# A diffusion-transformer block on one core: more dummy matmuls and wider scale matmuls ahead of the key projection, and a later gate load

## The chip, the cores and the metric

One core of a Trainium2 chip runs the whole kernel. The metric is the device time of one execution in microseconds; for a kernel the median of several runs is given. A profile is of one execution.

## The reference, cut to what matters

The block works on x (2 batches, 256 tokens each, width 1152) with a condition c (2 x 1152). All inputs are bf16.

```python
mod = (_silu(c) @ w_mod).reshape(B, 6, 1, D)
shift_a, scale_a, gate_a, shift_m, scale_m, gate_m = [mod[:, i] for i in range(6)]
h = _layernorm(x, axis=-1) * (1 + scale_a) + shift_a
qkv = (h @ wqkv).reshape(B, N, 3, H, Dh)
...
a = jnp.einsum('bhqk,bkhd->bqhd', attn, v).reshape(B, N, D) @ wo
x = x + gate_a * a
h2 = _layernorm(x, axis=-1) * (1 + scale_m) + shift_m
m = _gelu(h2 @ w_fc1) @ w_fc2
return x + gate_m * m
```

The change concerns scale_a (a product of silu(c), two rows, with a 1152 x 1152 part of w_mod), the key projection that follows it, and the load of the weights of gate_a.

## The kernel before, in words

Weights are cut into 9 slabs of 128 rows ("k-tiles"), tokens into 4 tiles of 128. Everything is recorded first as units with reads and writes; a small planner then gives each engine its order. The order of TensorE (pe) and of the DMA queue of SyncE (sp) is the order of the program text; DVE and ACT follow a list written by hand (`S.first`) at the start of the kernel and the planner's priorities behind it. Helpers record every operation: all ordinary matmuls stand on L692 (`mm`), all transposes on L695 (`tr`), all DMAs on L673 (`dma`), copies on L687 (ACT) and L689 (DVE).

The start of TensorE's order is:

1. `warm_a` (7 dummies), the transpose of c, `warm(5, "b")`. A dummy is a matmul of the identity with a zero tile of 512 columns into PSUM bank 2 (bank 7 for "a"); nothing reads its result.
2. `sca_one`: a matmul of ones that puts the 1 of (1 + scale_a) into PSUM bank 7 and bank 3. Then `sca_0`, `sca_1`, `warm(4, "c")`, `sca_2` to `sca_4`. `mod_kt` does one k-tile: for each of the five 128-wide column blocks f = 0 to 4 (`KC` = 5) it takes a 128 x 128 piece of the scale weights as the stationary operand and moves two columns, silu(c) of the two batches (`ST[:, kt:18:9]`, two elements 9 apart). Block 0 accumulates in bank 3, blocks 1 to 4 in bank 7. The other four blocks of scale_a come later, in unit `scb`, with the roles of the operands changed.
3. `xnT_1`, `xnT_0`: 9 transposes each of the normalised token tiles 1 and 0.
4. `sca_first`: block 0 for k-tiles 5 to 8; then DVE copies the first transposed k-tile (`xnT_cp0_0`) and multiplies it by the scale (`hk_0_0`, L831). Then `sca_5` to `sca_8` for blocks 1 to 4. `sc1a` (L819) copies the scales from PSUM to `SC1A`.
5. The key projection of batch 0: units `k0_<pair>_<k-tile>`, each two matmuls of 256 columns, k-tiles 0 to 4, with the transposes of tile 2 behind k-tile 1 and those of tile 3 (`xnT_3a`, `xnT_3b`) inside k-tile 4; then batch 1, `scb`, k-tiles 5 to 8, the shift (`sh`), the queries, scores, values, attention, the output projection and the MLP.

Token tile 3 is loaded behind the second key slab. DVE takes its statistics (L740, L741, L743), POOL its power (L744), and DVE normalises it in two parts (L771, 640 and 512 columns), which `xnT_3a` and `xnT_3b` read.

SyncE's queue holds, in order: x, the first scale weights (4 loads), key slabs 0 and 1, token tile 3, key slabs 2 to 4, the other scale weights (3 loads), key slabs 5 to 8, the shift weights (3 loads), then the query slabs 0 to 8 with the first gate load `ga_load(0)` behind slab 1, and what follows. The query slabs go where the scale weights were, so they wait for `scb`; the place of the gate weights (`WMODR`) is free from the start. DVE computes gate_a from them (`attn_gate`, L1061 for k-tile 0 and L1064 for the others); the result goes through a scratch buffer in DRAM and comes back as a row that L1165 multiplies with.

Of the kernel before, what the change touches and what calls it, by code (L numbers as in the profile page):

```python
# [497 lines left out]
P = 128  # L498
NTOK = 512
D = 1152  # L500
KT = 9
# [8 lines left out]
KC = 5  # L510
# [33 lines left out]
def build_kernel(nc, x, c, wqkv, wo, w_mod, w_fc1, w_fc2, out):  # L544
# [5 lines left out]
    with (  # L550
# [4 lines left out]
        def sb(off, nbytes, dt=BF16):  # L555
            assert off % 4 == 0 and off + nbytes <= ARENA_BYTES, (off, nbytes)
            v = arena[:, off // 2:(off + nbytes) // 2]
            if dt == F32:
                v = v.bitcast(F32)
            return v  # L560

        def ps32(bank, c0=0, n=512):
            return psum[:, bank * 512 + c0: bank * 512 + c0 + n]

        def ps16(bank, c0=0, n=1024):
            v = psum[:, bank * 512: (bank + 1) * 512].bitcast(BF16)
            return v[:, c0:c0 + n]
# [15 lines left out]
        def misc(nbytes):  # L583
            o = mo[0]
            mo[0] += (nbytes + 3) // 4 * 4
            assert mo[0] <= ARENA_BYTES
            return o
# [22 lines left out]
        Q4B = sb(O_Q4B, 1024)  # L610
# [21 lines left out]
        IDENT = sb(misc(256), 256)  # L632
        ONES = sb(misc(256), 256)
# [3 lines left out]
        ST = sb(misc(36), 36)  # L637
# [5 lines left out]
        SC1A = sb(misc(72), 72, F32)  # L643
# [27 lines left out]
        def dma(dst, src, nbytes, name, is_out=False, eng="sp", run=4096):  # L671
            eff = 1.0 if run >= 4096 else (1.08 if run >= 2304 else (1.15 if run >= 1536 else (1.3 if run >= 1024 else 1.42)))
            return S.op(eng, 500.0 if eng == "sp" else 150.0, lambda e: e.dma_start(dst, src), reads=[src], writes=[dst],  # L673
                        name=name, dma_bytes=nbytes * eff, is_out=is_out)

        def dve(cost, fn, reads, writes, name):
            return S.op("dve", cost, fn, reads=reads, writes=writes, name=name)
# [7 lines left out]
        def copy_on(eng, dst, src, n, psum16, name):  # L685
            if eng == "act":
                act(c_act(n), lambda e: e.activation(out=dst, in_=src, func=ACTF.Copy), [src], [dst], name)  # L687
            else:
                return dve(c_dve_psum16(n) if psum16 else c_dve_psum32(n), lambda e: e.tensor_copy(dst, src), [src], [dst], name)  # L689

        def mm(o, l, r, st, sp, **kw):
            S.instr(lambda e: e.matmul(o, lhsT=l, rhs=r, start=st, stop=sp, **kw), reads=[l, r], writes=[o])  # L692
# [62 lines left out]
        for t in range(4):  # L755
# [5 lines left out]
            m = MV[:, t, 0:1]  # L761
# [14 lines left out]
        def xt_ps(b, kt, n=1):  # L776
            if b == 0:
                return (4, 5, 6)[kt // 4], (kt % 4) * 256
            return (7, (kt - KC) * 256) if kt >= KC else ((6, 4)[kt % 2], kt // 2 * 256)

        def xn_T(t, part="", kts=range(KT)):
            b = t // 2
            S.unit("pe", len(kts) * c_mm(128), "xnT_%d%s" % (t, part))
            for kt in kts:
                bank, c0 = xt_ps(b, kt)
                tr(ps16(bank, c0 + (t % 2) * 128, 128), XN[:, t, kt * 128:(kt + 1) * 128], IDENT)

        def xn_T_copy(b, kts, eng):
            bank, c0 = xt_ps(b, kts[0])
            n = len(kts)  # L790
            src = ps16(bank, c0, n * 256).rearrange("p (k t) -> p k t", k=n)
            st = kts[1] - kts[0] if n > 1 else 1
            copy_on(eng, HX[:, kts[0]:kts[-1] + 1:st, b * 256:(b + 1) * 256], src, n * 256, True, "xnT_cp%d_%d" % (b, kts[0]))

        def warm(n, tag):
            for i in range(n):
                S.unit("pe", 215.0, "warm_%s_%d" % (tag, i))
                mm(ps32(2), IDENT, Q4B, True, True)

        def mod_kt(W, kt, col0, name, fs=(0, 9)):  # L800
            if name:
                S.unit("pe", (fs[1] - fs[0]) * 27.0, name)
            for f in range(*fs):
                mm(ps32(7 if f else 3, col0 + f * 2, 2), W[:, kt, f * 128:(f + 1) * 128], ST[:, kt:18:9], False, kt == KT - 1,
                   skip_group_check=True)

        def quads(w, g0, g1, q):
# [7 lines left out]
                   skip_group_check=not fresh)  # L815

        def sc1a(ka, kb):
            m, o = ps32(7 if ka else 3, 2 * ka, 2 * (kb - ka)), SC1A[:, 2 * ka:2 * kb]
            dve(170, lambda e: e.tensor_copy(o, m), [m], [o], "sc1a_%d" % ka)  # L819


        def hk(kt, b, eng="dve"):
            dst, s1 = HK[:, kt, b * 256:(b + 1) * 256], SC1A[:, kt * 2 + b:kt * 2 + b + 1]
            if kt + b == 0:
                s1 = ps32(3, 0, 1)
            bank, c0 = xt_ps(b, kt)
            src = ps16(bank, c0, 256) if kt < KC and kt + b > 0 else HX[:, kt, b * 256:(b + 1) * 256]
            if eng == "act":
                act(c_act(256, 1), lambda e: e.activation(out=dst, in_=src, func=ACTF.Copy, scale=s1), [src, s1], [dst], "hk_%d_%d" % (kt, b))
                return  # L830
            dve(256 if kt < KC else 200, lambda e: e.tensor_scalar(out=dst, in0=src, scalar1=s1, scalar2=None, op0=ALU.mult),  # L831
                [src, s1], [dst], "hk_%d_%d" % (kt, b))
# [10 lines left out]
        def k_pair(kts, i, b, bank=None):  # L843
            S.unit("pe", 2 * len(kts) * c_mm(256), "k%d_%d_%d" % (b, i, kts[0]))
            bank = KB[b][i] if bank is None else bank
            if kts[0] == 0:
                for kt in kts:
                    for half in range(2):
                        k_mm((kt,), 2 * i + half, b, bank, half)
            else:  # L850
                for half in range(2):
                    k_mm(kts, 2 * i + half, b, bank, half)
            if kts[-1] == KT - 1:
                eng = "act" if ev_rr[0] % 2 == 0 else "dve"
                ev_rr[0] += 1
                copy_on(eng, QK[:, 9 + 2 * i:11 + 2 * i, b * 256:(b + 1) * 256], ps32(bank).rearrange("p (j t) -> p j t", j=2), 512, False,
                        "k_ev%d_%d" % (b, i))

        warm(5, "b")
        S.unit("pe", 27.0, "sca_one")  # L860
        mm(ps32(7, 0, 2 * KC), ONES[0:1, :], ONES[0:1, 0:2 * KC], True, False, skip_group_check=True)
        mm(ps32(3, 0, 2), ONES[0:1, :], ONES[0:1, 0:2], True, False, skip_group_check=True)
        for kt in range(0, 2):
            mod_kt(WSC, kt, 0, "sca_%d" % kt, (0, KC))
        warm(4, "c")
        for kt in range(2, 5):
            mod_kt(WSC, kt, 0, "sca_%d" % kt, (0, KC))
        xn_T(1)
# [1 line left out]
        S.unit("pe", 4 * 27.0, "sca_first")  # L870
        for kt in range(5, 9):
            mod_kt(WSC, kt, 0, "", (0, 1))
        xn_T_copy(0, (0,), "dve")
        hk(0, 0)
        sc1a(0, 1)
        for kt in range(5, 9):
            mod_kt(WSC, kt, 0, "sca_%d" % kt, (1, KC))
        sc1a(1, KC)
        for kt in range(1, KC):
            hk(kt, 0, "act" if kt == 4 else "dve")  # L880
        xn_T_copy(0, (8,), "act")
        xn_T_copy(0, (5, 6, 7), "act")
        for kt in range(KC):
            for i in range(2 if kt == KC - 1 else 4):
                k_pair((kt,), i, 0)
            if kt == 1:
                xn_T(2)
# [15 lines left out]
        for c0, c1 in ((0, 32), (32, 32 * (KT - KC))):  # L903
            ka, kb = KC + c0 // 32, KC + c1 // 32
# [9 lines left out]
        def ga_load(k0):  # L914
            dma(WMODR[:, k0:k0 + 3, 0:FG], wmod_v[:, k0:k0 + 3, 2 * D:2 * D + FG], 3 * P * FG * 2, "ld_ga%d" % k0, run=FG * 2)

        for kt in range(KT):
            dma(WQ[:, kt, :], wqkv_v[:, kt, 0:D], P * D * 2, "ld_wq%d" % kt, run=2304)
            if kt == 1:
                ga_load(0)  # L920
        for kt in range(KC, KT - 2):
            for b in range(2):
# [225 lines left out]
        def acc_bank():  # L1148
            b = acc[acc_rr[0] % len(acc)]
            acc_rr[0] += 1  # L1150
            return b
# [125 lines left out]
        for t in range(4):  # L1277
# [4 lines left out]
            for (c0, c1) in pieces:  # L1282
                w = c1 - c0
                S.unit("pe", JT * c_mm(w), "fc2_%d_%d" % (t, c0))
                o = ps32(acc_bank(), 0, w)
# [22 lines left out]
def bass_standalone__dit_block__diffusion_kernel(  # L1308
    nc: bass.Bass,
    x: bass.AP,  # L1310
    c: bass.AP,
    wqkv: bass.AP,
    wo: bass.AP,
    w_mod: bass.AP,
    w_fc1: bass.AP,
    w_fc2: bass.AP,
    out: bass.AP,
):
    build_kernel(nc, x, c, wqkv, wo, w_mod, w_fc1, w_fc2, out)
# [28 lines left out]
```

## Time and profile before

| | |
|---|---|
| median of 3 runs | 242.92 us (242.85 to 243.38) |
| span of the profiled execution, first to last instruction | 242.5 us |
| time of the profiled execution around its span | not given by the page |
| TensorE busy | 237.3 us, 98% of the span |
| mean granted TensorE clock | 0.993 |
| DVE, ACT, POOL busy | 121.5, 67.8, 19.9 us |
| DMA | 51.58 MB, mean 213 GB/s |

Busy time of TensorE is the union of its matmuls, whose ends are modelled; neighbouring matmuls overlap in the records. The granted clock is the share of TensorE's full clock that was let through. A wait in the timeline stands in brackets behind the instruction that it held up, with what ended it.

### The profile page before, as it was taken

Reading aid. Unit: us, or ns where it says so; the run is one execution under the profiler, and the core shown is the slowest. Engines: PE = TensorE matmul, PEld = TensorE weight load, DVE = VectorE, ACT = ScalarE, POOL = GpSimd, SP = SyncE. Lnnn points to the kernel's source line nnn. Section 1 sums busy time; section 2 is a strip of 40 time slices with the busy share of each in tenths; the row PEclk is TensorE's granted clock in tenths of the full one; section 3 lists DMA queues with packets and bytes.
Section 4 is the critical chain, followed back from the end, with each engine's and each line's share of the span. In section 5 each row is a group of like instructions: output and inputs, shape, how many; then the busy total and the mean of one; then the engine's idle time right before and its main releaser. Section 6 shows DMA issues by size and latency. Waiting matters only on the chain.

```text
span 242.5 us, 3957 instructions
## 1 busy us (share of the span) xinstructions
PE 237.3 (98%) x1699; PEld 145.4 (60%) x1699; DVE 121.5 (50%) x229; ACT 67.8 (28%) x136; POOL 19.9 (8%) x36
## 2 busy tenths in 40 slices
PE   6899999999999999999999999999999999999995
PEld 2688844466666666898544444444666566566564
DVE  2654379988996689669999700000022222111112
ACT  4921440435524206973233322222000000000000
POOL 1300000000002276400000110000000000000000
PEclk9979999999999999999999999999999999999999
DMA  6999999999992999999963499100000000000000
GB/s 221 378 370 392 389 392 390 398 413 402 391 352 79 312 374 391 391 348 398 352 198 83 157 313 374 43 0 3 0 16 19 16 16 16 19 16 16 21 27 20
DMA packets 30363, 51.58 MB, mean 213 GB/s; under 512 B 1547, under 2 KB 15755, under 8 KB 30347
## 3 DMA queue, kind: packets, MB, share of 16 engines
q1 hardware_dynamic: 29888, 50.73, 58.9%
q0 software_dynamic: 288, 0.60, 0.8%
q8 instruction: 13, 0.21, 0.4%
q10 hardware_dynamic: 171, 0.01, 0.0%
q14 instruction: 3, 0.02, 0.0%
HBM read 50.15 MB, written 1.19 MB: 212 GB/s over the span
## 4 chain that ended last, share of the span: by engine, by line
PE 95%; DMA 3%; SPq 1%; DVE 0%; issue 0%
PE psum L692 93%; DMA arena<-in_wqkv_dram 3%; PE psum L695 2%; SPq L673 1%; DVE arena L1290 0%; DVE arena L1291 0%
## 5 line engine op out<-in xcount | busy, mean ns | idle before, releaser
L692 PE MATMUL psum<-arena 128*128 128x384 bf16 (+8 forms) x1610 | 234.0, 314 | 2.4 <-POOL arena L718 1.5
L692 PEld LDWEIGHTS psum<-arena 128*128 128x128 bf16 (+2 forms) x1610 | 139.7, 97 | 92.4 <-issue 3.8
L1290 DVE TENSOR_TENSOR arena<-psum,arena 128x384 f32<-128x384 f32 (+2 forms) x13 | 6.8, 526 | 88.6 <-PE psum L692 88.6
L1200 ACT ACTIVATE arena<-psum 128x512 bf16<-128x512 f32 (+1 forms) x45 | 22.8, 512 | 42.1 <-PE psum L692 42.1
L687 ACT ACTIVATE arena<-psum 128x512 bf16<-128x512 f32 (+6 forms) x34 | 18.2, 560 | 37.9 <-PE psum L692 37.9
L1064 DVE SCALAR_TENSOR_TENSOR arena<-arena 128x1152 f32<-128x1152 bf16 x16 | 21.9, 1408 | 0.0
L1095 DVE SCALAR_TENSOR_TENSOR arena<-arena 128x1152 f32<-128x1152 bf16 x16 | 21.4, 1414 | 0.0
L1166 POOL TENSOR_TENSOR arena<-arena 128x384 f32<-128x384 f32 x12 | 10.9, 912 | 11.7 <-DVE arena L1165 9.5
L740 DVE BATCH_NORM_STATS2 arena<-arena 128x6 f32<-128x384 f32 (+1 forms) x18 | 9.5, 549 | 3.8 <-DMA arena<-in_x_dram 3.8
L673 POOL DMA_DIRECT2D dit_scratch<-arena x4 | 2.4, 609 | 96.6 <-DVE arena L1082 60.3
L689 DVE CAST arena<-psum 128x512 bf16<-128x512 f32 x11 | 7.2, 687 | 5.3 <-PE psum L692 5.3
L1165 DVE TENSOR_TENSOR arena<-psum,arena 128x384 f32<-128x384 f32 x12 | 6.7, 556 | 3.7 <-PE psum L692 3.7
L1171 ACT ACTIVATE arena<-arena 128x1152 bf16<-128x1152 f32 x4 | 5.4, 1344 | 9.8 <-DVE arena L1170 9.8
L695 PE MATMUL psum<-arena 128*128 128x128 bf16 (+1 forms) x89 | 7.4, 225 | 0.4 <-DMA arena<-in_c_dram 0.4
L695 PEld LDWEIGHTS psum<-arena 128*128 128x128 bf16 (+1 forms) x89 | 6.3, 102 | 2.2 <-DMA arena<-in_c_dram 1.1
L1291 DVE TENSOR_TENSOR arena<-arena 128x384 bf16<-128x384 f32 (+2 forms) x13 | 6.9, 527 | 0.5
L1190 ACT ACTIVATE arena<-psum,arena 128x128 bf16<-128x128 bf16 x16 | 6.1, 455 | 3.0 <-PE psum L695 2.2
L1187 DVE TENSOR_SCALAR arena<-psum,arena 128x128 bf16<-128x128 bf16 x20 | 5.5, 336 | 2.9 <-PE psum L695 2.9
L1009 ACT ACTIVATE arena<-psum,arena 128x256 bf16<-128x256 f32 x8 | 3.7, 471 | 0.2 <-DVE arena L1006 0.2
L744 POOL TENSOR_TENSOR arena<-arena 128x1 f32<-128x1 f32 x6 | 3.3, 555 | 4.7 <-DVE arena L743 4.5
L1005 DVE TENSOR_REDUCE arena<-psum 128x2 f32<-128x512 f32 x4 | 2.8, 688 | 0.9 <-PE psum L692 0.7
L962 ACT ACTIVATE arena<-arena 128x256 bf16<-128x256 bf16 x6 | 2.5, 495 | 1.5 <-DVE arena L956 1.5
(60 smaller groups left out, 53.9 us busy)
## 6 DMA issues: line engine op xcount, KB each, us to landing
arena<-in_w_fc_dram SPq DMA_DIRECT2D x9, 1152.0 KB, 8.0
arena<-in_w_fc_dram SPq DMA_DIRECT2D x4, 2592.0 KB, 17.6
arena<-in_wqkv_dram SPq DMA_DIRECT2D x18, 288.0 KB, 9.3
arena<-in_w_mod_dram SPq DMA_DIRECT2D x6, 864.0 KB, 12.3
arena<-in_w_mod_dram SPq DMA_DIRECT2D x3, 1728.0 KB, 20.5
arena<-in_wqkv_dram SPq DMA_DIRECT2D x1, 2592.0 KB, 17.6
arena<-in_wo_dram SPq DMA_DIRECT2D x1, 2592.0 KB, 24.9
arena<-in_w_mod_dram SPq DMA_DIRECT2D x1, 2592.0 KB, 18.5
```

What stands on the lines that cost most here:

```text
L687: act(c_act(n), lambda e: e.activation(out=dst, in_=src, func=ACTF.Copy), [src], [dst], name)
L689: return dve(c_dve_psum16(n) if psum16 else c_dve_psum32(n), lambda e: e.tensor_copy(dst, src), [src], [dst], name)
L692: S.instr(lambda e: e.matmul(o, lhsT=l, rhs=r, start=st, stop=sp, **kw), reads=[l, r], writes=[o])
L695: S.instr(lambda e: e.transpose(o, i_, idn), reads=[i_, idn], writes=[o])
L740: dve(550, lambda e, s=s, o=o: e.bn_stats(out=o, in_=s), [s], [o], "bn_%s_%d" % (tag, ci))
L1064: ga_units[(b, kt)] = dve(150 + FG * 1.1, lambda e, o=o, w=w, s1=s1: e.scalar_tensor_tensor(out=o, in0=w, scalar=s1, in1=o, op0=ALU.mult, ...
L1095: u = dve(1300, lambda e, o=o, w=w, s1=s1: e.scalar_tensor_tensor(out=o, in0=w, scalar=s1, in1=o, op0=ALU.mult, op1=ALU.add), [w, s1, o], ...
L1165: dve(550, lambda e, o=o, ga=ga, x1c=x1c: e.tensor_tensor(out=x1c, in0=o, in1=ga, op=ALU.mult), [o, ga], [x1c], "wo_t1_%d_%d" % (t, ci))
L1166: S.op("pool", 930, lambda e, xs=xs, x1c=x1c: e.tensor_tensor(out=x1c, in0=x1c, in1=xs, op=ALU.add), reads=[x1c, xs], writes=[x1c], name=" ...
L1200: act(c_act(ntok), lambda e: e.activation(out=dst, in_=o, func=ACTF.Gelu_apprx_tanh), [o], [dst], "gelu_%d_%d" % (f, tok0))
L1290: dve(c_dve_psum32(w), lambda e, o=o, gm=gm, t1=t1: e.tensor_tensor(out=t1, in0=o, in1=gm, op=ALU.mult), [o, gm], [t1], "fc2_t1_%d_%d" % ( ...
L1291: dve(c_dve_32(w), lambda e, t1=t1, x1c=x1c, ost=ost: e.tensor_tensor(out=ost, in0=t1, in1=x1c, op=ALU.add), [t1, x1c], [ost], "fc2_out_%d ...
```

## The change

- In `mod_kt` each scale matmul moves 64 columns: the two columns of silu(c) repeated 32 times by a dimension of step zero. Each block f then has 64 columns of PSUM of which the first two are read. `sca_one` is widened to match, and `sc1a` reads two columns of every 64.
- `warm(4, "c")` becomes `warm(7, "c")`; one dummy goes into `sca_first`, behind k-tile 7 and ahead of k-tile 8; one (`warm(1, "d")`) goes ahead of the first matmul of the key projection.
- `ga_load(0)` is issued behind query slab 4 in place of query slab 1.

```diff
         def mod_kt(W, kt, col0, name, fs=(0, 9)):
...
-                mm(ps32(7 if f else 3, col0 + f * 2, 2), W[:, kt, f * 128:(f + 1) * 128], ST[:, kt:18:9], False, kt == KT - 1,
+                mm(ps32(7 if f else 3, f * 64, 64), W[:, kt, f * 128:(f + 1) * 128], ST[:, kt:18:9].unsqueeze(1).broadcast_to([P, 32, 2]), False, kt == KT - 1,
                    skip_group_check=True)
...
         def sc1a(ka, kb):
-            m, o = ps32(7 if ka else 3, 2 * ka, 2 * (kb - ka)), SC1A[:, 2 * ka:2 * kb]
+            m = ps32(7 if ka else 3, 64 * ka, 64 * (kb - ka)).rearrange("p (f c) -> p f c", c=64)[:, :, 0:2]
+            o = SC1A[:, 2 * ka:2 * kb].rearrange("p (f c) -> p f c", c=2)
...
-        mm(ps32(7, 0, 2 * KC), ONES[0:1, :], ONES[0:1, 0:2 * KC], True, False, skip_group_check=True)
-        mm(ps32(3, 0, 2), ONES[0:1, :], ONES[0:1, 0:2], True, False, skip_group_check=True)
+        ones64 = ONES[0:1, 0:64].unsqueeze(1)
+        mm(ps32(7, 0, 64 * KC), ONES[0:1, :], ones64.broadcast_to([1, KC, 64]), True, False, skip_group_check=True)
+        mm(ps32(3, 0, 64), ONES[0:1, :], ONES[0:1, 0:64], True, False, skip_group_check=True)
         for kt in range(0, 2):
             mod_kt(WSC, kt, 0, "sca_%d" % kt, (0, KC))
-        warm(4, "c")
+        warm(7, "c")
...
         for kt in range(5, 9):
             mod_kt(WSC, kt, 0, "", (0, 1))
+            if kt == 7:
+                mm(ps32(2), IDENT, Q4B, True, True)
...
         xn_T_copy(0, (5, 6, 7), "act")
+        warm(1, "d")
         for kt in range(KC):
             for i in range(2 if kt == KC - 1 else 4):
                 k_pair((kt,), i, 0)
...
             dma(WQ[:, kt, :], wqkv_v[:, kt, 0:D], P * D * 2, "ld_wq%d" % kt, run=2304)
-            if kt == 1:
+            if kt == 4:
                 ga_load(0)
```

## The prediction

> **What bounds the kernel now.** I read the page first: the busy line, the granted clock and the chain that ended last.
>
> ```profile
> span 242.5 us, 3957 instructions
> ...
> PE 237.3 (98%) x1699; PEld 145.4 (60%) x1699; DVE 121.5 (50%) x229; ACT 67.8 (28%) x136; POOL 19.9 (8%) x36
> ...
> PEclk9979999999999999999999999999999999999999
> ...
> PE psum L692 93%; DMA arena<-in_wqkv_dram 3%; PE psum L695 2%; SPq L673 1%; DVE arena L1290 0%; DVE arena L1291 0%
> ```
>
> TensorE carries 95% of the chain; the 3% in front of it is one transfer, the first key weights, landing at 10.76 us. After that PE never waits, so a microsecond taken from PE early in the kernel reaches the end, unless a transfer or another engine's result is not early enough. The clock row has one low digit after the start, a 7 in the third slice (12.1 to 18.2 us). I cut that region into equal stretches with the windows view (columns: length; PE busy and instructions; granted clock; DMA share; GB/s):
>
> ```profile
> 4.32:7.73 3.41, 2.96 (x23) 1.00 0.99 339
> 7.73:11.15 3.42, 2.67 (x58) 1.00 1.04 389
> 11.15:14.56 3.41, 3.41 (x22) 0.50 1.06 388
> 14.56:17.97 3.41, 3.41 (x40) 1.00 1.09 363
> ```
>
> From 11.15 to 14.56 PE has half its clock, and there it is busy without a break with K matmuls. Then PE's timeline (start, length, operation, count):
>
> ```profile
> 8.35 0.55 PE L692 MATMUL psum<-arena 128*128 128x2 bf16 x15 [0.53 <-DMA arena<-in_w_mod_dram]
> 8.76 1.17 PE L695 MATMUL psum<-arena 128*128 128x128 bf16 x18
> 9.76 0.88 PE L692 MATMUL psum<-arena 128*128 128x2 bf16 x20
> 10.81 3.31 PE L692 MATMUL psum<-arena 128*128 128x256 bf16 x16 [0.16 <-DMA arena<-in_wqkv_dram]
> 13.90 0.98 PE L695 MATMUL psum<-arena 128*128 128x128 bf16 x9
> 14.72 2.35 PE L692 MATMUL psum<-arena 128*128 128x256 bf16 x20
> 16.91 0.44 PE L695 MATMUL psum<-arena 128*128 128x128 bf16 x5
> 17.19 0.38 PE L692 MATMUL psum<-arena 128*128 128x256 bf16 x2
> 17.41 0.39 PE L695 MATMUL psum<-arena 128*128 128x128 bf16 x4
> 17.63 2.89 PE L692 MATMUL psum<-arena 128*128 128x256 bf16 x31
> ```
>
> Durations overlap, so costs come from start to start. At full clock: 2 columns (8.76-8.35)/15 = 27 ns; 128-column transposes (9.76-8.76)/18 = 55.6 ns; 256 columns (16.91-14.72)/20 = 109.5 ns; 512 columns 214 to 216 ns (the windows view has 187 records, two of them cut, in the 40 us from 125 to 165). At half clock, the 16 K matmuls from 10.81 to 13.90 are three at 109 ns and 13 at 212 ns.
>
> **Why the clock fell.** In time spent streaming columns, the stretch 4.32 to 7.73 holds nine 512-column dummies and the end of a tenth, 9 x 0.215 + 0.17 = 2.1 us, 62% of it, and the clock stayed. The stretch 7.73 to 11.15 holds 35 matmuls of 2 columns (35 x 0.8 ns = 0.03), 18 transposes (1.0) and three K matmuls (0.33): 40% with the transposes, 11% without. The clock then fell. What keeps it lies between 40 (or 11) and 62%.
>
> Whether transposes count no row separates, so I carry both sums.
>
> **The change, part by part.** *64 columns in place of 2.* No row has 64 columns. Bounds: 27 ns (2 columns) and 55.6 ns (128 columns). I take 29 ns: the step from 128 to 256 columns is 0.42 ns a column, so 64 are 26.9 ns, plus the 2 ns by which 128 columns exceed 53.8. There are 45 (10, 15, 4 and 16), so 45 x 2 ns = 0.09 us, part of it before a wait that hides it. The opening ones-matmul grows from 10 to 320 columns (0.14 us) and lies between 6.23 and 6.51, where PE waits for scale weights. The strided read of PSUM in sc1a stays 8 elements a row: nothing.
>
> *Three more dummies in "c"* (4 to 7): PE idles 0.53 us before 8.35 and its last dummy starts at 7.44. With sca_0 and sca_1 2 ns slower each, seven end at 6.82 + 7 x 0.215 = 8.33. The wait hides them; they would cost 0.65 us without it. *One among the first-column matmuls* (0.215): three of those go at once at 9.76, the fourth at 10.05, after its weights. Now it goes at 9.80 + 0.09 + 0.215 = 10.10. *One ahead of K* (0.215): 16 x 29 ns end at 10.60, the dummy at 10.82, and the K weights land at 10.76. The first column's user on DVE moves from 10.36 to 10.4 and is still done by 10.7. So K starts at about 10.83 in place of 10.81. The five dummies cost 0.02 us together because waits of 0.53, 0.2 and 0.25 us lie exactly there.
>
> *The clock.* The stretch 7.73 to 11.15 now streams 0.60 (dummies) + 0.43 + 0.215 + 0.58 + 0.215 + 0.33 = 2.4 us, 69%, and 99% with transposes. Both exceed the 62% that kept the clock, so I forecast 1.00 throughout.
>
> *K at full clock.* From 10.83: 16 x 0.1095 to 12.58; 9 transposes, 0.50, to 13.08 (their input on ACT ends 12.4, some 0.1 later now); the third key weights land at 5.35 + 7.7 = 13.05, the fourth and fifth at 13.8 and 14.5; 20 matmuls, 2.19, to 15.27. Next come the transposes of the last token tile, and here another engine becomes late:
>
> ```profile
> 14.08 0.15 DVE L743 TENSOR_SCALAR arena<-arena 128x1 f32<-128x1 f32 x1
> 14.89 0.77 DVE L771 TENSOR_SCALAR arena<-arena 128x640 bf16<-128x640 bf16 x2 [0.67 <-POOL arena L744]
> 17.39 0.87 DVE L831 TENSOR_SCALAR arena<-psum,arena 128x256 bf16<-128x256 bf16 x3 [1.73 <-PE psum L695]
> ```
>
> The first half of that tile is normalised at 14.89 + 0.45 = 15.34, after a chain that starts with X landing at 12.27 and does not move. With a semaphore PE goes on at 15.42: 0.15 us given back. Then 0.28, 0.22 and 0.22 to 16.14. Before, that point is 17.63: the gain is 1.49 us. (Half of 3.41 is 1.71; less 0.02, 0.15 and rounding.) The DVE row of 17.39 moves with the transposes.
>
> *What must be early enough for that gain.* The last scale weights land at 8.10 + 10.5 = 18.6 and are read in the last third of a stage that moves from 20.2 to 18.7; the sixth key weights at 19.4, wanted at 21.0; the last shift weights at 14.95 + 13.8 = 28.7, wanted in the last third of a stage moving from 30.1 to 28.6, so at 29.3 (the tightest, 0.6 us); the first Q weights at 29.5, wanted at 31.8. Nothing stops the gain.
>
> *Later first gate load.* On SP's queue it goes from behind the second Q load to behind the fifth, so Q loads 3 to 5 are issued earlier and the gate weights (864 KB, landed 21.44 + 11.1 = 32.5) land where the fifth Q load did, 23.81 + 10.9 = 34.7. It waits for nothing, so nothing queues behind it; POOL's queue is untouched. Its first reader, DVE L1061, ran at 35.12 and could run at 33.6; it will start at 34.8, holding back copies and softmax work queued behind it on DVE by up to 1.2 us. DVE's own waits for PE take that back: 0.51 us before 45.14 and 0.72 before 53.36. Price on the path: nothing; without that cover, the gate row would reach its first user (DVE L1165 at 81.59, row landed 80.6) 0.5 us late, with the four PSUM banks of that stage in rotation between it and PE.
>
> **Sum.** The profiled span is 242.5; the median of the runs is 242.92, 0.4 above, the part outside the span, which I leave alone. 242.5 - 1.49 = 241.0 of span, 241.4 of time. The three runs spread 0.5 us, and the profiled one has all of its half-clock stretch inside K, the dearest place; a stretch from 10.15 to 13.56 would cost (13.56 - 10.81)/2 = 1.4 us in place of 1.7. So the median may stand to lose a little less, and I take 241.5. The Trainium skill, "TensorE: Matmul & The Clock Gate", Part 1, says that the clock is halved after an idle window of 3.4 us and restored after a busy one, and that the window runs free of the kernel's start. The 3.41 us at 0.50 agrees; one trace cannot show the free running. By the rule the gain differs from run to run, about 1.0 to 1.5; without it, 1.5 in each.
>
> **Rivals.** *Half-speed operand (0.11).* The repeated operand is two elements 18 bytes apart, read by turns. If that streams at half rate, 64 columns take 55.6 ns like 128. Then sca_0 and sca_1 push the dummies past 8.35, all 45 are on the path, 45 x 27 ns = 1.2 us, and K starts at about 11.95; the wait of 0.15 vanishes, the second transposes' end is at 11.95 + 1.75 + 0.50 + 2.19 + 0.72 = 17.1 against 17.63: 242.4. Against it: nothing shown; for it: no contiguous row either. *Quarter speed (0.06), the slower side.* Same place: each at 107 ns costs 45 x 78 ns = 3.5 us, less the gain of 1.64 (no wait of 0.15): 244.8. It decides from about 65 ns a matmul (29 ns and 1.64 us over 45) and is slower beyond 0.2% from 76 ns. The bound is the 128-column row doubled, 111 ns. The Trainium skill, "Advanced Engine Details and Errata", "SBUF Cachelines", speaks for both: an access that goes to another 16-byte line each time pays a penalty, of no stated size; no run here shows it. *The clock falls all the same (0.09).* If activity is counted otherwise (array cells or useful weights), 0.50 stays in the row and only 0.03 us is added: 242.95. For it: the exact threshold is unknown; against it: 69% against a kept 62%.
>
> **How the numbers follow.** The main case has 0.74. About 0.2% (0.49 us) is what a measurement of this kernel can tell from no change, so faster is below 242.43. The half-speed case straddles that: 0.06 of it is faster, 0.05 is same. Faster 0.74 + 0.06 = 0.80; same 0.05 + 0.09 = 0.14; slower 0.06. The range goes from 241.1 (all 1.71 gained) to 242.6 (half speed with 0.2 more), holding 0.85.
>
> **What would show it.** Right: the clock at 1.00 from 11.15 to 14.56; K's first row at 10.8 to 10.9; 64-column starts 29 ns apart; a PE wait of 0.1 to 0.2 us near 15.3 for DVE; the 31-matmul row near 16.1; L1061 at 34.8. Wrong: 0.50 anywhere in K, a K row near 12, or a new PE wait behind 20 us.

## The result, and the profile after

The changed kernel takes 244.68 us (median of 4 runs, 244.62 to 244.92); the kernel before takes 242.90 (4 runs). The ratio is 1.0074, 95% interval 1.0061 to 1.0088: slower by 1.8 us, where 1.4 us faster was forecast.

With this result came, for each run, its time and its span side by side. The profiled execution of the changed kernel has a span of 243.2 and a time of 244.92; time less span is 1.7 to 1.8 us in every run of both kernels since. So the trace that the prediction was made from, with its span of 242.5, is one of an execution of about 244.25 us, and not of the 242.9 us that it was set beside.

The windows view of the changed kernel, in the same stretches as before (length; PE busy and instructions; granted clock; DMA share; GB/s):

```profile
4.32:7.73 3.41, 3.04 (x12) 1.00 0.97 322
7.73:11.15 3.42, 3.42 (x43) 1.00 1.04 381
11.15:14.56 3.41, 3.36 (x45) 1.00 1.05 393
14.56:17.97 3.41, 3.41 (x40) 1.00 1.09 360
```

This trace holds no clock record at all, so none of its four 1.00 says anything, and only 12 instructions stand in the first row. The half-clock stretch in the key projection (K) is gone all the same, as forecast: its 16 matmuls up to 14.91 follow each other by 109 ns, where 13 of them took 212 ns before. PE's timeline of the changed kernel (start, length, operation, count, wait):

```profile
4.98 0.19 PE L695 MATMUL psum<-arena 18*128 18x18 bf16 x1 [0.29 <-DMA arena<-in_c_dram]
5.10 5.63 PE L692 MATMUL psum<-arena 128*128 128x512 bf16 x39
10.57 1.17 PE L695 MATMUL psum<-arena 128*128 128x128 bf16 x18
11.57 3.51 PE L692 MATMUL psum<-arena 128*128 128x64 bf16 x37
14.91 0.67 PE L695 MATMUL psum<-arena 128*128 128x128 bf16 x9
15.42 2.35 PE L692 MATMUL psum<-arena 128*128 128x256 bf16 x20
17.60 0.44 PE L695 MATMUL psum<-arena 128*128 128x128 bf16 x5
17.88 0.38 PE L692 MATMUL psum<-arena 128*128 128x256 bf16 x2
18.10 0.39 PE L695 MATMUL psum<-arena 128*128 128x128 bf16 x4
18.32 0.93 PE L692 MATMUL psum<-arena 128*128 128x256 bf16 x7
```

There is no wait longer than 0.15 us between 5.1 and 18.3: the waits that were to hide the dummies are gone, and PE is late. Transposes start at 10.57 (8.76 before), K's first matmul is at 13.17 (10.81), and the row forecast near 16.1 is at 18.32. From K's first matmul to that row it is 5.15 us (6.82 before): K does run at full clock. From start to start the 64-column matmuls are 58 to 60 ns apart, not 29.

### The profile page after: what moved, and what is told of

It is laid out like the page before. It is cut to its first block, busy times and chain, and to the rows that moved or that the text cites. A ratio compares the mean times of both kernels' runs of the same rounds, so it can differ in the third digit from the quotient of the medians.

```text
span 243.2 us, 3958 instructions
## 1 busy us (share of the span) xinstructions
PE 238.3 (98%) x1695; PEld 146.5 (60%) x1704; DVE 121.3 (50%) x229; ACT 67.8 (28%) x136; POOL 20.2 (8%) x36
## 4 chain that ended last, share of the span: by engine, by line
PE 96%; DMA 2%; issue 0%; SPq 0%; DVE 0%
PE psum L692 94%; DMA arena<-in_w_mod_dram 2%; PE psum L695 2%; SPq L673 0%; DVE arena L1295 0%; DVE arena L1296 0%
## 5 line engine op out<-in xcount | busy, mean ns | idle before, releaser
L687 ACT ACTIVATE arena<-psum 128x512 bf16<-128x512 f32 (+6 forms) x34 | 18.3, 560 | 39.0 <-PE psum L692 36.8
```

## Experiments

Times are medians; behind each stands the ratio to the kernel before, run beside it on the same chip, with its 95% interval. The letters of theories and rivals are those of the expectations. "Ones" is the matmul of ones ahead of the first scale matmul. Starts of single matmuls are read from the trace, where the rows shown merge several.

**e5_before: the kernel before, for a trace of its usual execution.** No edit.

> The kernel before, unchanged, for a trace of its usual execution. In the comparisons so far 33 of 35 of its executions have a span of 240.9 to 241.6 and two 242.6 to 242.7, and time minus span is 1.7 to 1.8 in all; the trace that the prediction was made from has 242.5 and belongs to the two. Theory F (the trace shown was of a rare execution): K starts near 10.8 us with 109 ns between matmuls from the first to the last, no half-clock stretch behind 8 us, and the last pair of the first batch's K at 16.2 to 16.4, not 17.6; span near 241.2. Rival G (the shorter spans come from somewhere else, later loads or the end): the half-clock stretch is there and the pair stands near 17.6.

243.19 us (1.0007, 0.9988 to 1.0026). The traced execution has a span of 241.4 and a time of 243.20. PE's timeline in it:

```profile
8.72 1.17 PE L695 MATMUL psum<-arena 128*128 128x128 bf16 x18
9.73 0.86 PE L692 MATMUL psum<-arena 128*128 128x2 bf16 x20
10.78 1.03 PE L692 MATMUL psum<-arena 128*128 128x256 bf16 x8 [0.19 <-DMA arena<-in_wqkv_dram]
11.99 1.03 PE L692 MATMUL psum<-arena 128*128 128x256 bf16 x8 [0.18 <-DMA arena<-in_wqkv_dram]
12.86 0.67 PE L695 MATMUL psum<-arena 128*128 128x128 bf16 x9
13.51 2.36 PE L692 MATMUL psum<-arena 128*128 128x256 bf16 x20
15.83 0.45 PE L695 MATMUL psum<-arena 128*128 128x128 bf16 x5
16.12 0.38 PE L692 MATMUL psum<-arena 128*128 128x256 bf16 x2
16.34 0.39 PE L695 MATMUL psum<-arena 128*128 128x128 bf16 x4
16.56 2.68 PE L692 MATMUL psum<-arena 128*128 128x256 bf16 x23
```

K starts at 10.78 and runs at 109 ns throughout; the row that stood at 17.63 is at 16.56, a little behind the expected 16.2 to 16.4 because the second key weights landed late (the wait of 0.18). Theory F holds. Over all the comparisons of this study, 121 executions of the kernel before, 10 show the mean clock 0.993 and spans of 242.5 to 243.1; the others have spans of 240.9 to 241.8 (for four only the time is on record, at most 243.38). The trace of the prediction was of the ten.

**e1_dummies: the dummies and the gate load, 2 columns as before.** Against the changed kernel (`sca_one` and `sc1a` go back with it):

```diff
-   mm(ps32(7 if f else 3, f * 64, 64), ..., ST[:, kt:18:9].unsqueeze(1).broadcast_to([P, 32, 2]), ...)
+   mm(ps32(7 if f else 3, col0 + f * 2, 2), ..., ST[:, kt:18:9], ...)
```

> The five dummies and the later gate load, with 2 columns in the scale matmuls as before. Theory A (the 64-column operand costs 60 ns in place of 27 and spends what the clock gives): no such cost here, the dummies lie in waits, so K starts at 10.8 to 11.0 us. If the dummies alone keep the clock at 1.00, the span falls by about 1.5 to 241.0 and the time to about 241.4; if it takes the 64 columns to keep it, the K matmuls stay 212 ns apart for 3.4 us and the span is about 242.5. Rival B (the dummies themselves are what costs, inside the span or outside it): K starts 0.5 us or more later than 10.8, or the time stands 1.7 us over the span as in the changed kernel (before: at most 0.9), and the time is 243.5 or more.

243.11 us (1.0006, 0.9993 to 1.0018); span of the trace 241.1. K starts at 11.05, a little behind the expected 10.8 to 11.0, and its counterpart of the 17.63 row is at 16.20. The span is what theory A said, the time is not: 241.4 was worked out with 0.4 us outside the span, and it is 1.7. Against the usual execution of before there is nothing to gain, and the dummies cost about 0.15 us or nothing.

**e2_cols64: 64 columns alone.** The edit of the change in `mod_kt`, `sca_one` and `sc1a`, on the kernel before.

> 64 columns in the scale matmuls, no extra dummy, gate load as before. Theory A: 60 ns from start to start; 15 of them from 8.35 end at 9.25, the transposes at 10.25, 20 more at 11.5, so K starts near 11.5 in place of 10.8; with PE streaming all that time the clock holds, K is done 1.5 us quicker, the span is about 241.8. Rival B (dummies cost): this kernel is the faster part of the change, time below 242.4. Rival C (the wide operand brings time outside the span): time minus span is 1.7 here too, and the time is 243.5 or more.

243.52 us (1.0019, 1.0004 to 1.0035); time less span is 1.7 here as everywhere, which ends rival C. From its timeline:

```profile
8.65 1.06 PE L692 MATMUL psum<-arena 128*128 128x64 bf16 x15 [0.17 <-DMA arena<-in_w_mod_dram]
9.55 1.17 PE L695 MATMUL psum<-arena 128*128 128x128 bf16 x18
10.55 3.08 PE L692 MATMUL psum<-arena 128*128 128x64 bf16 x36
```

(9.55 - 8.65)/15 = 60 ns. The 20 behind the transposes take 1.2 us, so K starts at 11.73, 0.95 us behind the usual 10.78; half of that is given back by waits in K that are no longer needed.

**e3_gate: the later gate load alone.**

```diff
-            if kt == 1:
+            if kt == 4:
                 ga_load(0)
```

> Only the first gate load moved behind the fifth query load. Theory A: within 0.2 us of before; DVE's first gate instruction starts near 35.1 as before. Rival D (the gate load costs): slower by 0.5 us or more, with a wait of DVE or of PE behind 35 us that before does not have.

242.95 us (1.0000, 0.9986 to 1.0014). Nothing, as forecast for this part. The traced execution happens to be this kernel's slowest, 244.18, and shows a second way to lose over a microsecond: c landed late, its transpose is at 5.68 (5.03 in e5), the dummies behind it stay 0.43 us apart until about 9.8, and K starts at 12.44 and runs at 109 ns.

**e4_pair: the whole change, with the two values of silu(c) side by side.**

```diff
-   ... ST[:, kt:18:9].unsqueeze(1).broadcast_to([P, 32, 2]) ...
+   ... ST[:, 2 * kt:2 * kt + 2].unsqueeze(1).broadcast_to([P, 32, 2]) ...
```

(`c_silu` writes in that order, and the other readers of `ST` follow.)

> The whole change, but silu(c) is stored with the two batches side by side, so the 64 columns alternate between two neighbouring elements (2 bytes apart) in place of two that are 18 bytes apart. Theory A, cost by the distance: 29 ns from start to start, K starts near 10.9, the span is about 241.0 and the time 241.4. Rival E (cost of a repeated operand, step zero, whatever the distance): 60 ns as in the changed kernel, K near 12.2 or later and the time near 244. Rival C (time outside the span comes with the wide operand): time minus span 1.7.

243.30 us (1.0012, 1.0000 to 1.0024): 1.4 us better than the change. From start to start 31 ns. The repetition by a zero step costs at most the 2 ns above the forecast 29; the distance did. The span of 241.0 and the time of 241.4 that theory A expected were missed (241.5 and 243.30, K at 11.47): the time, as in e1, because there was no half-clock stretch to win back.

**e6_cols32: the whole change with 16 repeats.**

```diff
-   mm(ps32(7 if f else 3, f * 64, 64), ... broadcast_to([P, 32, 2]) ...
+   mm(ps32(7 if f else 3, f * 64, 32), ... broadcast_to([P, 16, 2]) ...
```

> The whole change with 32 columns (16 repeats) in place of 64. Theory A1 (about 0.9 ns for each column that lies 18 bytes from the one before it): 29 to 33 ns from start to start, nothing left of the cost, time near 243.3 as with neighbouring elements. Rival A2 (a fixed price of about 30 ns for such an operand, whatever its length): 45 to 60 ns, time 244.2 or more.

33 ns from start to start, 243.22 us (1.0006, 0.9989 to 1.0022). The price is per column: (59.5 - 33)/32 = 0.83 ns, twice the 0.42 ns of a 256-column matmul.

**e9_dist8 and e10_dist16: the two values 8 bytes apart in one 16-byte line, and 16 bytes apart.** As e4_pair, with `ST` wider and aligned to 16 bytes.

```diff
+   e9:  ST[:, 8 * kt:8 * kt + 5:4]        e10:  ST[:, 16 * kt:16 * kt + 9:8]
```

> The whole change, with the two batches of silu(c) 8 bytes apart inside one 16-byte line. Theory M (the price is for going to another 16-byte line): 31 ns from start to start, time near 243.3 as with neighbours. Rival N (only neighbouring elements stream at full rate): 45 to 60 ns, 244.0 or more.

> The whole change, with the two batches 16 bytes apart, each at the start of its own 16-byte line. Theory M and rival N both: 60 ns as at 18 bytes, time as the changed kernel. If it is 31 ns, both are wrong and the price at 18 bytes is for something else, such as the odd offset.

e9: 31 ns, 243.31 us (1.0006, 0.9993 to 1.0018). e10: 58 to 60 ns, 244.21 us (1.0045, 1.0029 to 1.0062). Theory M holds as far as it was tried: two elements in one 16-byte line are cheap, two in different lines dear. Two elements under 16 bytes apart but astride a line's end were not run, so a price by distance, from 16 bytes on, is not ruled out. e10 has the change's spacing, but stayed 0.55 us under its time. In the traces that lies at the front alone: from the first scale matmul to K it is 5.57 us in e10 and 5.59 in e11, but the first scale matmul is at 6.98 in e10 and at 7.43 in e11.

**e7_c4 and e15_c5: the whole change with four and with five c dummies.**

```diff
-        warm(7, "c")
+        warm(4, "c")        (e15: warm(5, "c"))
```

> The whole change with four dummies in the c group in place of seven; the 64 columns and the two single dummies stay. Theory H (the slow operand pushes the dummies out of the waits that would hide them, so that each then costs its 0.215 us): faster than the whole change by 0.4 to 0.65, near 244.1. Rival I (dummies cost nothing, all 1.8 us are the operand's): no difference, 244.7.

> The whole change with five c dummies in place of seven. Four gave 243.7, seven 244.7. Each dummy at 0.215 on the path: 0.43 below the whole change, 244.3; theory Q lets the place of the clock's rise move that by up to 0.4 either way between executions, so a spread from 243.6 to 244.6. Rival R (a step between four and seven, such as weights that are waited for): either 243.7 or 244.7, not between.

e7: 243.70 us (1.0027, 1.0011 to 1.0044). e15: 243.76 us (1.0011, 0.9984 to 1.0038; that run of before had 243.23). So the dummies do cost once the operand is slow, but three of them took 1.0 us off the median and not 0.65, and two took as much as three, which is what rival R said of five dummies. The traces part the dummies from the rest. From the first scale matmul to K it is 5.59 us with seven (e11), 5.29 with five (e15, with a wait of 0.13 for scale weights behind them) and 4.96 with four (e7): three dummies cost 0.63, as theory H had it. The rest of the medians' difference lies ahead of the first scale matmul, which starts at 7.43, 6.64 and 7.58 in these traces; that of e7 is of its slowest execution, 244.33.

**e11_after: the changed kernel again.**

> The changed kernel again, unchanged, beside its variants on one chip. Theory H (operand slow, so the dummies stand on the path): with four c dummies it took 243.7, three more on the path add 3 x 0.215 = 0.65, so 244.35; no execution in the slow-clock group. Rival L (something else belongs to the whole change and not to its parts): 244.6 to 244.9 as first measured, with a term of 0.3 to 0.5 that the parts do not show.

244.77 us (1.0064, 1.0043 to 1.0086), on another chip. The 0.4 us that the parts don't show is real (rival L). The traces of the change and of e15 differ at the very front, in the row of the five b dummies. PE's timeline up to the matmul of ones (start, length, operation, count), first the change, then e15:

```profile
5.10 2.13 PE L692 MATMUL psum<-arena 128*128 128x512 bf16 x5
```

```profile
5.17 1.26 PE L692 MATMUL psum<-arena 128*128 128x512 bf16 x5
```

The same five matmuls take 0.87 us more in the change. They start 0.40 to 0.43 us apart there, and the matmul of ones follows at 7.16 (7.16 in e11 too); in e15 it follows at 6.36. PE's clock had not yet risen from its first, half speed. In the traces of this study that hold a clock record it rises between 4.3 and 7.4 us, and by the spacing in e3 only near 9.8.

**e13_no_b: the whole change without the b dummies.**

```diff
-        warm(5, "b")
```

> The whole change without the five b dummies. In the traces TensorE's clock rises from half to full at a place between 4.3 and 7.4 us that varies; where it is late, the five b dummies take 2.1 us in place of 1.1 and the first scale matmul starts near 7.4 instead of 6.6. Theory Q (with the slow operand and the extra dummies no wait is left ahead of K, so a late rise reaches K in full, and this is the 0.4 us that the parts did not show): the first scale matmul starts at 6.4 to 6.9 in the trace, K about 0.6 to 0.9 earlier than 13.0, median 243.9 to 244.2. Rival R (the remainder belongs to the three extra c dummies): 244.5 to 244.8 as the whole change.

Median 245.25 us (1.0065, 1.0028 to 1.0102), but in two groups: two of six executions at 243.94 and 244.08, as theory Q said, four at 245.25 to 246.25, two of those with a clock record of 0.992 and 0.993. The traced one is of the first group: ones at 6.28, K at 12.18, 0.84 us before e11's. So time lost at the front does reach K in full in the changed kernel; and without these dummies the clock is lost in other executions. The two at 246.06 and 246.25 read 1.00, which can mean no record; no trace of them was kept, and the expected median of 243.9 to 244.2 was missed.

**e8_no_c: the kernel before without its four c dummies.**

```diff
-        warm(4, "c")
```

> The kernel before without its four c dummies. Theory J (the clock is halved when a stretch of 3.4 us at a place that varies from execution to execution holds too little matmul work; in the kernel before only a narrow range of places qualifies, so 2 of 35): far more of the executions, a third or more, have spans near 242.5 and times near 244.3, the rest stay at 241.2 and 243.0. Rival K (the slow executions of before have nothing to do with PE's work, a hiccup of the chip): still about 1 in 17 and the median 242.9 to 243.0.

244.09 us (1.0031, 1.0002 to 1.0059), spread from 242.93 to 245.67. Seven of 12 executions show clocks of 0.993 or 0.986 and times from 243.97 on, five are at 242.93 to 243.12. Theory J holds. The windows view of the traced one (time 245.67):

```profile
5.77:9.18 3.41, 1.97 (x35) 1.00 0.98 332
9.18:12.59 3.41, 3.05 (x43) 0.50 1.04 392
12.59:16.01 3.42, 3.42 (x21) 0.50 1.08 373
16.01:19.42 3.41, 3.41 (x39) 1.00 1.07 376
```

Two stretches of 3.41 us at half clock, beginning 9.18 us into the kernel where the prediction's trace had 11.15: the edges lie on a grid of 3.41 us that is not tied to the kernel's start.

**e12_pair_only and e14_pair_b2: 64 columns from neighbours, nothing else of the change; and that with two b dummies.**

> The kernel before with 64 columns from neighbouring elements and nothing else of the change: no extra dummies, gate load as before. Theory A: 31 ns in place of 27, 45 x 4 ns = 0.2 us, half of it in waits; K starts at 10.8 to 11.0; median 242.95 to 243.15, and no execution with a half-clock stretch in K. Rival O (64 columns cost for another reason, such as writing 64 columns to PSUM): 243.4 or more. Rival P (columns do not keep the clock): still about 1 execution in 13 near 244.4.

> The kernel before with 64 columns from neighbouring elements and two b dummies in place of five. Theory Q: the front of the kernel no longer depends on where the clock rises, K starts at the landing of its first weights in every execution, and the 64 columns keep the clock: median 242.8 to 243.0 and a highest run below 243.5. Rival S (the b dummies are needed to raise the clock): K matmuls 212 ns apart for a stretch in some executions, runs at 244 or more.

e12: 242.96 us against 243.02 (0.9994, 0.9981 to 1.0007), 12 executions from 242.53 to 243.45, none with a half-clock stretch. Its spacing, from two rows:

```profile
9.34 1.17 PE L695 MATMUL psum<-arena 128*128 128x128 bf16 x18
10.34 0.78 PE L692 MATMUL psum<-arena 128*128 128x64 bf16 x20
11.38 1.91 PE L692 MATMUL psum<-arena 128*128 128x256 bf16 x16 [0.26 <-DVE arena L822]
```

Twenty in 0.78 us with the last one's tail; a wait of 0.26 is still left ahead of K, which starts at 11.38 and not at the expected 10.8 to 11.0 (the clock rose at 7.39 here). The median is that of the kernel before. That its rare half-clock stretches are gone is not shown by this run alone: at 10 in 121, about one draw of twelve in three would have none. e14: 243.49 us against 243.23 (0.9997, 0.9969 to 1.0025), runs from 242.99 to 243.96: no better, and theory Q's bound of 243.5 was missed.

## Why the prediction was wrong

Two steps failed: the base of the sum, which turned the forecast gain of 1.4 us into nothing, and the price of the 64 columns, which with what hung on it made the kernel 1.8 us slower.

*The base of the sum: the first failing step.* "242.5 - 1.49 = 241.0 of span, 241.4 of time" took the 0.4 us between the profile's span and the median for the part outside the span. That part is 1.7. The profiled execution had a time near 244.25; the half-clock stretch, all in K, was in it and in 10 of 121 others. In the usual execution there was nothing for the change to win: e1, which has the dummies without the operand, ends this stage of K where it was forecast (16.20 for 16.14), has the forecast span (241.1 for 241.0), and has a time no better than before. The sum's "1.49 us" is right for the rare executions (242.7 against 241.2 of span) and is worth 8% of itself, 0.12 us, on the average. The prediction noticed that this execution had "the dearest place" and that the runs spread by 0.5 us, and took 0.1 us off. It had the fact that speaks against it: a stretch that costs 1.4 us would spread the runs by more than 0.5 if it came and went, and if it never went, no run could be at 242.85 with 1.7 us outside its span; but that 1.7 was not on the page.

*64 columns: the second failing step.* "I take 29 ns", between 27 and 55.6. Measured 59.5, beyond the upper bound, which was a contiguous 128-column row; e4 and e9, with both values in one line, have 31. The rival "half-speed operand" had the mechanism and the place (all 45 on the path, dummies pushed past 8.35, K near 12); at 0.11 it was given too little. Here the Trainium skill's rule that speaks against the change, "Advanced Engine Details and Errata", "SBUF Cachelines", agrees with e4, e9, e10: within a 16-byte line 31 ns, across lines 58 to 60.

*The dummies at 0.02 us together.* True with a 2-column operand within 0.15 us (e1). With the slow one, the waits named as cover are used up, as the prediction's rival said.

*The way to 1.8 us.* Between the trace of e5 and that of the change, K starts 2.39 us later: about 1.43 of operand (45 matmuls, 59 ns on the mean and not 27); 0.45 of c dummies (1.51 us where 1.06 with its wait stood); the two single dummies nothing beyond the waits in their places (0.43 of dummies for 0.18 and 0.33 of waits, so 0.08 given back); and 0.60 at the front, where the first scale matmul starts at 7.57 and not 6.97. K then takes 5.15 us and not 5.78, since the waits inside it are gone: 0.63 back. 2.39 - 0.63 = 1.76, against 1.8 between the medians.

*The 0.60 at the front* is 0.31 of ones that start later (7.16 and 6.84), from a late rise of the clock; 0.11 of the wider ones, which take 0.15 us where 0.04 stood and which the prediction had put into a wait; and 0.18 of a longer wait, in the change's trace alone, for the first scale weights (landed at 7.52; 6.69 in e11). The usual kernel absorbs a rise as late as this: with the ones at 6.23 and at 6.84 its K starts at 10.81 and at 10.78. It has its limit too: with the ones at 8.05 in e3, K starts at 12.44. The changed kernel passes it on (e13, and e10 against e11). Why all nine of its executions, on two chips, look like late ones, while those of e15 and most of e7 and e10 do not, is not settled.

*The clock.* The forecast that the change keeps it is right: of 113 executions of kernels with the extra dummies or the wide operand and at least two b dummies, none has a mean clock under 0.999. As 1.00 can also mean no record, the times have to bear it out, and they do: none lies more than 0.63 us above its kernel's median, where the ten of before with a half-clock stretch lie 1.2 to 1.6 above theirs. The reading that too little streamed work lets it fall is supported by e8, which does not tell it from more waiting, since the same edit lengthens a wait of PE to 1.44 us. The upper bound of "40 (or 11) and 62%" comes down for the reading without transposes: in e5 the stretch from 6.22, where its clock rose, to 9.64 holds 1.4 us of dummies, 41%, and the clock stayed.

*The gate load and the wait for DVE.* Nothing, and nothing, as said. The wait of about 0.13 us near 15.7 stands in e5, not in the change, which is later than DVE there.

## What to carry to other kernels

Before a loss seen in one profile is priced, ask whether the median runs have it: the profiled execution's own time beside its span and the spread of the runs decide, and a clock stretch is the first suspect for being there in some executions only. A filler that keeps TensorE busy must cost nothing itself: check that its operand does not go to another 16-byte line with every column, and that the waits that hide it are still there after every other edit of the same change. Slack ahead of a critical stage also absorbs what varies from run to run; a kernel that fills it with work gets slower by more than the work.

## What the runs showed of the hardware

- A moving operand (the one whose columns stream through the array) that goes by turns to two elements in different 16-byte lines streams at half rate, 0.83 ns a column where 0.42 is usual: 64 columns at 16 or 18 bytes take 58 to 60 ns, at 2 or 8 bytes inside a line 31 ns, 32 columns at 18 bytes 33 ns. A zero step by itself costs at most 2 ns in 31.
- TensorE's clock is granted in stretches of 3.41 us whose place against the kernel's start varies (edges at 11.15 in one trace, at 9.18 in another, the first rise between 4.3 and 7.4 us in the traces with a record). The Trainium skill, "TensorE: Matmul & The Clock Gate", Part 1, says that the window runs free; the traces agree. A stretch can be halved behind one in which PE was far from idle: in 7.73 to 11.15 of the first trace it was busy for 2.67 of 3.42 us, with 2-column matmuls and transposes for the most part.
- A granted clock of 1.00 in a view can mean that the trace has no record of it. The dummies 0.43 us apart, where 0.215 is full speed, show half clock in the change's first row all the same, and in e3 up to about 9.8 us.
